# The last boot pass of V through the ordinary staging tiles, in the first one-layer steps, with a new instruction order

## The chip, the cores and the metric

One core of a Trainium2 chip runs the whole program. The metric is device time in microseconds (us), from one launch. The engines are PE (TensorE, matrix products), DVE (VectorE), ACT (ScalarE), POOL (GpSimd) and SP (SyncE, which here only issues transfers). DMA queues move data between HBM (device memory) and SBUF (on-chip memory); PE writes its results into eight PSUM banks.

## The reference

The input x has 2048 rows of 512 numbers. Two layers of attention with a recurrent memory (A) and a gated feed-forward (B) follow each other, both with the same weights:

```python
for s in range(n_seg):                       # 64 segments of 32 rows
    h = concat([mem, xs])                    # 8 memory rows and the segment's 32
    q, k, v = h @ Wq, h @ Wk, h @ Wv         # 32 heads of 128
    p = softmax(where(mask, q @ k.T * scale, -1e9))
    o = (p @ v) @ Wo
    mem = o[:8]                              # goes into the next segment
    outs.append(o[8:])
...
x = x + A(layernorm(x)); x = x + B(layernorm(x))   # B: (sigmoid(x Wg) * (x Wu)) Wd
x = x + A(layernorm(x)); x = x + B(layernorm(x))
```

## The kernel before

The memory rows make the 64 segments a chain. The kernel runs it in 70 steps: step t does segment t of layer 0 and, six steps later, segment t - 6 of layer 1, so that from step 6 to step 63 two layers share a step. Steps 0 to 5 have layer 0 alone and steps 64 to 69 layer 1 alone; these are the one-layer steps. A block is four segments; after each block of layer 0 its feed-forward (`ffn`) runs beside the steps, and its result feeds layer 1.

A step (`emit_step`) forms q and k for three heads at a time (L820), copies them out of PSUM, forms scores (L855), does the softmax in six groups of heads on DVE and ACT (L869 to L886: mask, maximum, subtraction, exponential, sum, reciprocal, product), transposes the probabilities (L898), multiplies with V (L925), and adds all heads through Wo in one bank (L943). The eight memory rows of the result go by a DVE copy (L961) into the tile hT of the next step, whose q and k wait for them. While there is no second layer, the first steps also form some columns of q and k for layer 1 in advance and save them through HBM (L849).

V does not depend on the memory for the rows of x, so it is formed in passes over 128 rows (`v_pass`, L609): eight pieces of 512 columns, each four 128x512 matmuls into one bank, a copy of the bank into a staging tile by ACT (L1176) or DVE (L1178), and writes of the staging tile to a scratch tensor `scr` in HBM (issued at L1172). A step reads its rows of V back into `vsb` (L789). What depends on the memory is formed in the step by strips (L734) and sent to `vsb` by L800. In an ordinary pass (`boot=False`) a piece goes to one of three tiles `vst` of 512 columns, and its writes are SP's. In a boot pass (`boot=True`) two pieces share a tile of 1024 columns from `bootp`, which borrows the nine ring tiles of the feed-forward weights (wd, wg, wu); its writes may go through SP or POOL, and the first loads of feed-forward weights wait for them (key "boot"). Seven boot passes of V, 56 pieces, run before and during step 0, for blocks 2, 14, 3, 4, 5, 7, 8, 10, 11 and 13 (`v_group`). The other blocks' rows of V come in beside the steps.

Boot also loads 16 MiB of weights (L496), whose transfers are issued by SP in one order with the rest of SP's work. SP and POOL have eight completion semaphores each: a transfer that takes one of them again waits for the one eight places earlier.

Nothing decides the order at run time. Every operation is recorded as a task with its dependencies; a packed table, `SEQUENCE`, gives the order of all tasks and, for tasks that may run on ACT or DVE (or SP or POOL), the engine. Then `replay` walks through this order with a table of costs, gives out tiles and banks, and sets the points of PE's work that the weight loads wait for; `warm` puts filler matmuls (L1162, on a tile of zeros) into PE where the plan leaves PE a gap over 250 ns near the start or in a stretch that is thinly filled with work.

Other lines of the profile: L569 transposes after a layer norm, L1013 the transpose ahead of a feed-forward, L1045 its gate and up products, L1068 its down product, L647 a half pass of V in boot.

Of the kernel before, what the change touches and what calls it, by code (L numbers as in the profile page):

```python
# [19 lines left out]
P = 128  # L20
MEM = 8
SEG = 32
L = MEM + SEG
# [3 lines left out]
NE = 14  # L27
# [26 lines left out]
;AzM!%Uu8nfB)KXVa0!tyA+v$awbu4`Kb`sD&qBM7uk$l2<aL9R`6B!jm=p6C^4)G&-1V@N>?u=U;*vtxzQ{<%y2d&u9DJ)U9CcRnC$6K!ij29MjC|~4KeQ93};?JQ7p@p1l)J*i!4g7+Bml0$ycMF-5YDdE_tMsZML)~cd?  # L54
}nJGL{`SyyT7;{fQ?*qBj!X1w_q9_L9p+-_rEfj(2^Qi4-0L<fxa6hdMklb>T@5A|k}ehjQ*{y5i=kgF8o(d{{O7GdF@Kj;J4s1vz-S*j?l1!WQ3b2G2#3Z{Rh*nyGO1@R-f_wKK51jA@8qwD~dF5X8VnzD0=Fe^+#pmy5m;
LUi$9=bhyZw14pl*t)pF}ga8SI9>}jO$Ym5Z_z(=ubg^h?&XJ1|QqZq_cZzLuzy#y;0H49pL`DshQU5fBlQ9Icc(z#Kb(Fa8W`fTYBvCvpLQ6*2e?+3ae9A(Nx;AUJ7YQxP8m$>Q-~uH~*4AYD><bXVJFPH4gH2_bXA!f424
@_r#~~-gm}MW;UejiWp{aJ)hi+l<6Ygrtd;7TKwO!xBySu(XZCrMjF7u`VA8t(jR!J{zR48z@Aiz$Lx>u=+Da|Nd@Jl@C!f9e6$s2{=Bom3p1|oAKY+p+<pV&Q?LU`v_4TZTh(Y*7k{uTw~)t889>{(ro!SoMr>PYU15#msZ
_}t+ek9rur<9#IIr?bpIJH!kkm1`@DI$;_#upVyKMH=^*}z36l&bjqmxJr<2*;@Y&`>sORISXA?*4Kh9}6>clU~Q*(Ztx-1Jo^LiJ>2)99=JGEZs{pR9wj?m6fv{5u6yJ=7B^Cg2-DU*XDS*q4ueJ*wl#L0OuF3gnn2@I2W|
I|9NbCrGR{Jip%xBqiFuV!Bf$3M6;LjF=W~UJH<g7`i1VZsE@R51DQH=IuLCb0}H4MUuI$tk4{EQMv@7i|pXc7{od_bJ!Z;@A?LZUj6-~nJg^Vw(q5xhy>fv4)%eRgl;}7W1feO6xvgFOVo@{Q<g$S!T41ZYWD8X{RWev3Zy
Ryh1AKtZJ}*M_d~*clQv!?_O(LhFXy4^Qy{g%b)re${{`K14VW+80jW^+%|bLlIPN{3#$&3*iV$hcYnMKO!1J+2V2B1-?Nwzxa@r+Mm#a>F?%b_X0C(3ljxJ!j7@`4ot+NL;c>g(MRO9?aJFC3a2Ho_!g$sV{WYL?Dkal!XV  # L60
@+^^eEU8<s#XnQjX*dw-{8J<gnvo|+_`w`?W7wu&vlEO%YqB(OaA}fFr87cMohwR1MpZ^*xOT0#NJhLsn&T>0d5v<eo!!}8XV9CdnF=U9mjeEnL!4(d7yZ_ybuRghPRU61x0_vQN?a;z1ZW7fSPMM?R0|&Xal0odTIy)MUXz
!bvxg-Ou0A5;&?tJxBc#?w=~3THxeKX1EHJ+?AzCG1r?&dIc$K9BsxIj9Zcc#LFncBB%GRpQ)KxBVCx|g-ENCrklW{MH*^IEXc_4`1V-jREC${Q3`gH*^=;P7?|&0H+hM>-HkZ{W%ztPn=z^-pEI7t?>6h+vGqOr6Rvuy4ft
40nPc@$uPvEosQ2Y|)nIKXK&rh{I&Uox}Xp@l}ND@z;eQp@H`^4M?0si?|>FM7a?7yYnOurV4#EoGevdai_XMK~SBs;eeQ5~(9z-V({bt18AG~n!isTDl8Msk-c0ADjgC0C3*@Lwuq0C>(sD}rOMj{g`;D(bSEs)wuVmckUp
47ma*F*bKwFl>YscB(?TVKo(g3kksEi%iB^E1;z@>i7Q%vz8u+FW?iy<}5d+I3sgF%xP^!tZnw|V-q;3=hAT82qj4r&re;vxN)T-GCRM$yI3WX!~7VHvgH!`8$?Y}G%kFMxT7_r*m89mwn(T&iKVdqcbmG|hgSzj_5|g{OJc
R(5d9!S3u|k+d&!DQb-K44Pe7Y`5o#evpE&KVqp*p4myYjmV`Gd3d{OPFkFJ*f=l;RVz1IB+&uXZK%RxX1!}UsW5X1gnspCdb`l4k*4T(kICd;vH3Zyr~Eq5|)@v=}{IAR{b+8@TVaS$JT+H&`VT<A*-9$4)n2zyJt+TqV^%
&r8W@^zu2WI>;NZiq15vYQx0;<C)fwd-H1a-`+j`h7}-l3x1|C9g`OGsFGRJN2yvDUU^Kx7u%@nR*J!6forss36zR+~{<;1WM(#<emy&6Jk$&m?iDL7Tt1<*)QN?B0mQ~3gQ+tNr{~(0b`g4<9N<DmOQEtE9G?A&A9q@Z3+`
#@HHeP5*_V#W%tQF#8^3A@APVUvQb0w=$uax&HuCqWt{+-5wWpr4@v{s-GYDc^^df-s41ZzUxpa{uQtm>FNGR!{g5n-VUB|x2@eZC>;+ubkKjE3D>|FuN;&;f@@Zs4MwdCIwVhk#=2eawi%w8jh$O(XZ{5TJk!25T4pgdm#m
zm54B6Y{`mGUuXP3*KW0w-P)f)#nXX@|I%cdQTW4tUYmtjn`()Uj3zf4HoC=Em|0y~KitYRDX24EI`drN7z>9+(;&Q^CzHl1#J=;DP{?QfsTEI+}7I3^z#zt>mq>j>+t_?66QS1nXMY@Ad_=HTt2jFm8~wA60Dvbny8*u3CN
8XmnU?X+LwX3ui2zXnF`bSu+yn5T>7>HT2<GC(Z5pXRTMs8w`PC)?$nA`3?3oz-KmdaQ(;env^f8ps5q7lkRR14}KCC_Mn2jAAn>TdiihS&6`L!3u_e6IYY62rL=CFm`8@T(gS^rBAYX<|x~<2RPtw`4{~KQOJ5GHc$W}Y`i
RRZg;<&k{>$m$cuPAft<?N+IN}Vahdk5Q+39I?~+x7E0~X0qV(0-T1l@{jg+^S@`^Bl%4!l}TCayYFH6GRY8?{1vu3oPUVbY74a2#l2r8Xg50WFBwe(4nGfp+799}_x-JxrZ5RMv<ciRxtB2;k6dDuo4>0zxTtyRY^+KE~<i  # L70
Y7eAJ3J{5XDKorFD&=Nbp{3pDcYUlE*1Go1~q@8ilQQ6I{-q!Z)KHnVYIV?3F9r!IdpY$NBlUNS}U5r8S3)IqMesa1o?qe)u&ujG6qY$<K|2mHo3)fU&RN&s5e_K7O{=_9z6UkN2K9ViA^krjvD$Irv;^oiMEUlbI-=G*Fp|
)3lv(5@bmv6cKn`3?%<$pV}@=g&$a@nlS=nHJZgg2)AlXrc*mV!#bQ(%j(}7p{wKV7Q7e*!pVj0WQ*OEEgKiaV8TV5+)?P7Y=y)P@lkOCdGucw4MhU|(y_Z~%W3TJGeTs#8Z&87JcrRX6(b>2pz0W>V|3}`d3{CRTSfQ;fNC
u%8OyxIJ89R~d<fCY3jx=~fe%avFoU-+!EP4A-)7Q7hl%Ak<D?&|yAD?78YFi=Ac$dc1K>5Mp(vOcS8u-P<_+}J^I3dWDopUxmaB~dOpw@l+>AUfT%Lm+Z4_XU@#p5|93`O^5+4{PHUPyDfasia4jqzozHQ6IHVAr|pHp1OV
mr!C?Dt8(P0bHn3oPsfsUZyANxTC-WGyIxKf}sEVJo{x*1A4O`O3Q<6YM9zEKRPeNZ^-nCG%z|oN;}h1PV2mVONn6Do_z+E90fa8`6s4t67mjA25kEvYYqo)6Jz|@kWdDOWHynvJraE`0gKYEnak+p#fPw;1qKRHk5Ou}(Sn
V78>^6>fFK2PqQ!(4_pN{&{C<s-n!<+1Vu#NOZf6z4wW3gqVMlBM`Vy>KnmLBZ_b4cYwMJj!P_p#FxX^SeZbO0|ac2YW)}8m*|N63&qv@DOra9i@?5l*njGHeZY9zmBwxku>Atv2FYO{ZHgDCof$X`@$subc&<5thxNrEePt
AudIJfh2W!CdP_KLPV5>~6>mN=!JEjZ_^?Y4!p<>BDvZL+O<jN@f00Mu1b^hSWR~6@mm4O7_>Gcc&a7X$#2Fw$)a)5L-Z314z8D+I0KfCFsQ+=2?YpWLhK#y{2Ia!JS+=Lm6mTw2xO;3FHvm5`34FeI-#B@A2z?wYX=ARxw_
tuU8@k{fr{Sv#bo>Ks?jgSsjAv`4DFOKn#VKjcu1tDl6w&PU|^<tJP?A&5l$ttcM6ID_N9j;;<WhQiw4_LXSBOeX11wz`70FI;cFy8~DROxYvx`b@MGwNs#1bU&pyd#a+<Xs3R#iO52d=-AB*d#Y^Aso1Jez3|PMaRj#COH;
j$tHfy;ya4~ZKc>T=`3oJwkZeD=T;z@<u{owk44ldXh%2iR6r&W231gX5+c0{M)49=*|_YDUr6-f~?YYbz0>pb}X5N5;XR0uSqAoxgU&`4^zJ}AFvfTW-Jl^DejXZ%iCCo_fxf4)pQY^8L6vDJ$x!?4Q;NqOKdbR}llga}&Q
@eZf>iaIQTN$S6A1e(DeM3KXW9R$jeJRw**TZS_+ZHJ0SCKRm;RU(r?51y~gO#_UJ=AvfX<CODs?AzSp#2@Jw8Weh;`Xw05k|8w%kWeWBkb(PDladC&@8Xi_At?H$TVx_1VDRzcNW#H3=pPLqZ{@V;3r6^idU9=U2QDycoCa
}X<;9E#ct(Zl!i5Ah`!104t8F2UlGY-aWLUe36yGaoQi9HIJIS~ZBtpEL_gL{cRne-!yMVsnL%kUF1tjZNAA(o!hj4mte1`ZPSs_ZWjP25@@Xc*@bg|<JslWe(&UFAz{yV(Lc&=-k{l0+Rw(aML&yWGi@U=v05n!X~4dEHN3  # L80
m95IPR`Aoo1;&d;XHy#!rlQZy}j#{(5htjIUq?0uP)lrfl7+`Xt4^f&W((|J(a!~11KdUbe3#G9ecttYzELIl@`Y_t-(t<57??;gSqPhA~-b$>FH;;&G8u6xHN+)OAn_aeS74l%s`TV1#otgP4`uCbaYkS*$wYD#-JIqA_P0
#1J5g+)l8UK7?&!3NizPK&S215c-|HTih11x?l3$m)#n7wLgw-7oQ#IyuKGzx8WyOf+DtpQ&s%y&PD(|r#(rw@s?44YCP$bJ0Po<HriBC3R~Qq|dRO-XA8y9ZQfC%)osl)<i&be@gKqatZK>(u4_|U@U<WWn#-tE*68Zi+<~
;sa1ky6+J{9Vj*YtYD3Tt)pzA^(E|HNwv6y2U8ZsLTHjF|=Zf#%6UkV<WLhOd;+Z1&F`_)t8ROVo_&EahI7xPY-GgQ(!n!|W=fn`Il6EGc?ngbb8FQ7?@xKhnyoC_e-?&*%>hY+>=|4yCasgBKR&8H+%LzD~kzqWwfXGsqD*
?1%6y!A8@Td&;#;U^SZ1^N`4T@)Z&3;oK(flk;5-c^%X^j!*~r4YY=jW5m#XE$QyDcWw*LEx%fv895eWw7Yg_JAe2rJhkz{ATZ&QGu`;*diH=ydnsA$BkIXPb^6p~(mz<j7rz9^k15#?N#N6qQKskAG85E>aB`r-2shNeRov
e=IMOZvfHg1t?EQ(of^BmUiwl<K!np`>y0se`d%^yn?f9+=kDcWb)XlTYcB~xTMlN@*-|wXZjJ%ki&MXd8-&bsOEoA5Mh=p+pjF^;rf~#WB@#nMKrVD!xV7&4&D1n8$nFJ&CGe;C$wyV=SHb)RQ7O_q|Q@xx{Ps>4B3)h|6Y
Z4*#cO$R)(t|Z|z<zv}FKZijIBcTHKjMi%CzRpCI;@mBit1}-SlP!sowvv`H!5$|qNK5RR*#~^EJtME+S!-vgll!5;7j9of>#1|$&IV(q0}(K0)sQ=4LW!&MFa&r0;Uxeu;;mC!|cEZnU*bjIQ&f{yTR-xadAP_4Ib+^s95P
558E(H5{&c2T7Vlh;oarLxWPacTwuKjuWPWSE}sFh(-J#V*T0QX`*Ar=g60>)+ZiXR>?W_ToSBx{&14#k;wm;Iu8@EosGYaBl$*NdM|rPTgeaoTEr?vIU*H`xIid@#h=%j@<6HkDB+Kn}-98p0+e?4=Z5CRdv6CB_XbTjB5U
i;}kKO-8kmg>@5<06G+sXnrIg9gV*mMFaZ5)2%F#q|fSNs8rv%-FcJ}LT<AyXtgYqV9~kUlxD{K_<Z5OVN0wLP?r0w+o4$Ze}~=Z9EMT7=yafzJusmAclbmz9TVpx~#`vb~@c{6GCIPz#{5y{+O6O50(IMNCIX+QI|IW_&SO
+te<Jgv>W3qhxtF<GhYBL?nVPgR|y>D>OZ})C3O_v;K<xYY~YB4pMPJ!saxrKUBmxQT)=o-U{cLdZO_U*uJPcA~$ypL_N#}E(GsT5!;fM;qOw=rP4MLGNYpawv#r=L}xfb_!<o(0__lO$V$<rWtLQKeML$J9(H0D5b@okfJm
LES-?xAA)ICmEgnLGL2Ul!9UZy@y*WXTv3Bp$1h-JP+cOEo>%Ghw39pQz(Hl|z@B6F`#Z&Q!Ff*#RIk|5#J~^mcX*5LeCV^p@j}JGOh3ppQeYTcZh##M1<W&f6*NS+K$<MymH5=zc|9)(`tWuiH>qc;C0s(g4ydoAm9ocdsu  # L90
;LR{N_AMqOq=@oM8DrR!sgqeF-~OAjvL4g!KI6e9EACK@~P*agJEaZcW~e4_g&w{EC031XLA70canUmHw@;xlOwboX6=wI@uapuHXE@9rZ}xZU#sn=%?P28Jd(X;oxMRenVnh^aq58De*FrUhT#$8Ze8~j$V%L+Y8SbR?c+7
Z#4_9Ze)n&=%)B9--_JpaimP1;FuCL1#!tCui?Y7;ocEmktl;)FYiKOz)R#;1RAHC;eR29gRrS-S{bIuNOxeoCn<BQ$tmbGFmKmANEb@O9=Ygqp+=ImkN?T;Oc?>fEm@LsGkuJy{3zYwQs@lnOTs1a^3FzYDfoz&Vs^Zmf{>
;>pp_mo7DJ5s4U~tlD`EC6<9m8$QSg?avq59L1S~Bv7w54MR3?$roWel+*c+#5N32_StS<|WhnK>XowbHXmAfQm*-XUY8hGQJRKFvg)Pw1HLCt!=mpp6zVv-tp(rEnQYbg_%zUX+@@{R(_gmDolu3KKHH3r`(T_z*{N8=VrA
#5^o2td_E)Gh&vJyBwFP5mG631|UN2le{`l6!>&1t~PiE{kEZ|Ho}f@y@W7{OPQC{dpR?sk8_c72tT>UnZ}dk8!xv5CyCidpIwTQ(R%s}R(&=#Hd*#(J60srdqHBaR<NGi;*r8tDhV28{~tCo!ZT`YTG_NJ)dhT)%$)^nvh<
# [266 lines left out]
class Kern:  # L361
# [312 lines left out]
    def v_group(self, blocks, psts, cuts):  # L674
# [5 lines left out]
        for b, cut in zip(blocks, cuts):  # L680
# [3 lines left out]
            for q, c0, r0, nr in cut:  # L684
                xi = (base + q) % 2
# [556 lines left out]
```

## Time and profile before

| | |
|---|---|
| median of 3 runs | 1766.37 us (1762.68 to 1766.64) |
| profiled execution, its own time | 1766.95 us |
| span in that profile | 1765.1 us |
| matmuls / weight loads recorded | 39831 / 40045 |
| granted TensorE clock, mean | 1.00 |
| bytes moved | 273.42 MB, mean 155 GB/s |

The page's first part gives each engine's busy time. A PE that is busy is not a PE at its peak: matmuls are pipelined, the ends are modelled, and fillers count as work. Rows of 512 columns have a mean of 379 ns each, but in a run of such matmuls one starts every 0.216 us; so a stretch's useful work is found from what runs of equal matmuls take, not from the mean of one. In the chain of waits each line gives the start in us, the duration in us and what the end of the program depended on at that time. A line such as "issue" means that the engine waited for nothing that the profile shows.

### The profile page before, as it was taken

What the parts mean: (1) busy time and instruction counts of PE and PEld (TensorE: products, weight loads), DVE (VectorE), ACT (ScalarE), POOL (GpSimd) and SP (SyncE); (2) the same over time, 40 slices, a digit from 0 to 9 for tenths busy, and PEclk for the clock granted to TensorE, in tenths of its full rate; (3) what the DMA queues carried; (4) which work ended last, traced back from release to release, by engine and by line L of the source; (5) the groups of instructions that cost most, each with busy time, mean ns of one, the idle gap of its engine ahead of it and who ended that gap; (6) DMA issues with size and microseconds to landing.
All of it is one profiled execution on the core that took longest, in us unless ns stands there. A gap on an engine that the chain in (4) does not pass through costs nothing.

```text
span 1765.1 us, 92070 instructions
## 1 busy us (share of the span) xinstructions
PE 1735.9 (98%) x39831; PEld 1505.6 (85%) x40045; DVE 1244.9 (71%) x4136; ACT 1103.3 (63%) x2906; POOL 573.8 (33%) x825
## 2 busy tenths in 40 slices
PE   9999999999999999999999999999999999999998
PEld 4588888889898888989898888988888898989887
DVE  5677677767677766776677778667766776677775
ACT  4576766566556656666666656656665666666564
POOL 4413032422333242323333242333324231333433
PEclk9999999999999999999999999999999999999999
DMA  9935364644555464545556464555456553554544
GB/s 310 313 81 140 103 173 134 180 137 132 161 150 164 134 175 143 152 123 158 170 141 175 125 181 112 156 160 160 141 144 178 147 155 111 162 160 140 171 127 118
DMA packets 135480, 273.42 MB, mean 155 GB/s; under 512 B 30730, under 2 KB 68498, under 8 KB 135074
## 3 DMA queue, kind: packets, MB, share of 16 engines
q0 software_dynamic: 56032, 181.39, 35.4%
q1 hardware_dynamic: 79042, 86.14, 17.0%
q8 instruction: 314, 5.14, 1.3%
q14 instruction: 92, 0.75, 0.1%
HBM read 221.78 MB, written 27.07 MB: 141 GB/s over the span
## 4 chain that ended last, share of the span: by engine, by line
PE 89%; DMA 4%; DVE 3%; SPq 2%; issue 1%; ACT 1%; DVEq 0%; POOL 0%; ACTq 0%
PE bank L820 31%; PE bank L943 17%; PE bank L1045 11%; PE bank L734 7%; PE bank L609 6%; PE bank L925 4%; PE bank L855 4%; PE bank L1068 4%; PE bank L898 2%; DMA wk_sb<-in_A_Wk_dram 1%; SPq L800 1%; DMA vsb<-sst 1%; PE bank L569 1%; SPq L496 1%; DVE st L869 1%
## 5 line engine op out<-in xcount | busy, mean ns | idle before, releaser
L820 PE MATMUL bank<-hT,wq_sb 128*128 128x80 bf16 (+3 forms) x8960 | 615.7, 198 | 3.0 <-issue 1.8
L820 PE MATMUL bank<-hT,wk_sb 128*128 128x80 bf16 (+3 forms) x8960 | 615.5, 198 | 2.5 <-issue 1.2
L1176 ACT CAST qku<-bank 128x480 bf16<-128x480 f32 (+3 forms) x770 | 383.8, 507 | 247.0 <-PE bank L820 218.5
L820 PEld LDWEIGHTS <-wq_sb 128*128 128x128 bf16 x8960 | 452.7, 99 | 32.3 <-issue 17.1
L820 PEld LDWEIGHTS <-wk_sb 128*128 128x128 bf16 x8960 | 447.0, 99 | 3.1 <-issue 1.8
L869 DVE TENSOR_TENSOR st<-bank,cst 40x240 f32<-40x240 f32 (+3 forms) x768 | 280.5, 368 | 129.1 <-PE bank L855 110.4
L943 PE MATMUL bank<-otsb,wo_sb 128*128 128x80 bf16 (+1 forms) x8960 | 362.8, 198 | 2.4 <-DMA wo_sb<-in_A_Wo_dram 1.3
L943 PEld LDWEIGHTS <-wo_sb 128*128 128x128 bf16 x8960 | 334.6, 99 | 11.1 <-DMA wo_sb<-in_A_Wo_dram 1.4
L1038 POOL DMA_DIRECT2D wu<-in_B_w_up_dram x217 | 164.6, 759 | 331.4 <-PE bank L1045 83.6
L1062 POOL DMA_DIRECT2D wd<-in_B_w_down_dram x217 | 154.2, 711 | 349.2 <-PE bank L855 102.6
L1176 ACT CAST otsb<-bank 128x480 bf16<-128x480 f32 (+3 forms) x420 | 201.1, 483 | 94.8 <-PE bank L925 62.8
L1037 POOL DMA_DIRECT2D wg<-in_B_w_gate_dram x217 | 164.3, 757 | 230.4 <-PE bank L1045 93.5
L879 ACT ACTIVATE st<-st 80x240 f32<-80x240 f32 (+3 forms) x420 | 159.1, 381 | 79.3 <-DVE st L876 76.8
L1045 PE MATMUL bank<-xnT,wg 128*128 128x128 bf16 (+2 forms) x1784 | 171.7, 218 | 1.0 <-issue 0.2
L1045 PE MATMUL bank<-xnT,wu 128*128 128x128 bf16 (+2 forms) x1784 | 171.2, 218 | 0.2 <-issue 0.2
L881 DVE TENSOR_REDUCE small<-st 80x6 f32<-80x240 f32 (+3 forms) x420 | 151.4, 362 | 23.8 <-ACT st L879 21.2
L855 PE MATMUL bank<-qku 128*128 128x80 bf16 (+1 forms) x2240 | 164.5, 197 | 1.1 <-ACT qku L1176 0.2
L876 DVE TENSOR_TENSOR st<-st,small 80x240 f32<-80x240 f32 (+3 forms) x420 | 154.7, 370 | 5.9
L886 DVE TENSOR_TENSOR pb<-st,small 80x240 bf16<-80x240 f32 (+3 forms) x420 | 153.7, 370 | 6.4
L874 DVE TENSOR_REDUCE small<-st 80x6 f32<-80x240 f32 (+3 forms) x420 | 152.1, 364 | 6.6
L925 PE MATMUL bank<-ptsb,vsb 104*128 104x80 bf16 x2048 | 140.6, 199 | 3.3 <-DMA vsb<-sst 0.9
L1051 DVE SCALAR_TENSOR_TENSOR hff<-th,bank 128x256 bf16<-128x256 f32 (+2 forms) x231 | 93.0, 403 | 62.8 <-ACT th L1049 62.3
(107 smaller groups left out, 2331.7 us busy)
## 6 DMA issues: line engine op xcount, KB each, us to landing
wg<-in_B_w_gate_dram POOLq DMA_DIRECT2D x220, 256.0 KB, 4.3
wu<-in_B_w_up_dram POOLq DMA_DIRECT2D x220, 256.0 KB, 4.2
wd<-in_B_w_down_dram POOLq DMA_DIRECT2D x220, 256.0 KB, 4.0
vsb<-scr SPq DMA_DIRECT2D x460, 48.0 KB
vsb<-sst SPq DMA_DIRECT2D x464, 32.0 KB
scr<-vst SPq DMA_DIRECT2D x112, 96.0 KB
wv_sb<-in_A_Wv_dram SPq DMA_DIRECT2D x8, 512.0 KB
wo_sb<-in_A_Wo_dram SPq DMA_DIRECT2D x10, 384.0 KB
```

Source lines behind the costliest of these rows:

```text
L820: nc.tensor.matmul(o_ap, lhsT=W[:, c, h * P:(h + 1) * P], rhs=mv(c), start=(c == 0), stop=(c == DC - 1))
L855: nc.tensor.matmul(s_all(SB)[:, w0 + i, :], lhsT=fview(qku[:, i, 0, 0:1], [(1, P)]), rhs=qku[:, i, 1, 0:ncol], start=True, stop=True)
L869: pl.add("DVE", dve_ns(n, True), lambda gsz=gsz, hs=hs, st=st, SB=SB, pj_=pj_, npj_=npj_, mk=mk, idx=idx: nc.vector.tensor_tensor(out=st[p ...
L876: pl.add("DVE", dve_ns(n), lambda gsz=gsz, hs=hs, st=st, mx=mx: nc.vector.tensor_tensor(out=st[pr, hs], in0=st[pr, hs], in1=mx[pr, hs].uns ...
L879: pl.add("ACT", act_ns(n), lambda hs=hs, st=st: nc.scalar.activation(out=st[pr, hs], in_=st[pr, hs], func=ACTF.Exp, scale=self.scale), r=s ...
L925: nc.tensor.matmul(fview(OB[:, o:o + 1], [(ncol, 2), (1, L)]), lhsT=self.vsb[halves[u // 8]][0:64 + L, j, (u % 8) * P:(u % 8 + 1) * P], rh ...
L943: nc.tensor.matmul(WB[:, c * ncol:(c + 1) * ncol], lhsT=self.wo[:, h, c * P:(c + 1) * P], rhs=otsb[:, hl, 0:ncol], start=(h == 0 and c == ...
L1037: pl.add("POOL", 760, lambda wg=wg, fs=fs: nc.gpsimd.dma_start(out=wg[:], in_=self.wgv[:, :, fs]), r=[("wo", self.H - 1)], w=[gk] + bt, la ...
L1038: pl.add("POOL", 760, lambda wu=wu, fs=fs: nc.gpsimd.dma_start(out=wu[:], in_=self.wuv[:, :, fs]), r=[("wo", self.H - 1)], w=[uk] + bt, la ...
L1045: nc.tensor.matmul(gu[:, 2 * i + k, 0:n], lhsT=W[:, c, i * P:(i + 1) * P], rhs=xnT[:, c, rw], start=(c == 0), stop=(c == DC - 1))
L1062: pl.add("POOL", 760, lambda wd=wd, ip=ip: nc.gpsimd.dma_start(out=wd[:], in_=self.wdv[:, 2 * ip:2 * ip + 2, :]), w=[dk] + (["boot"] if se ...
L1176: nc.scalar.copy(out=dst, in_=src)
```

## The change

The third pass of the last boot group (its rows come from blocks 11 and 13) becomes an ordinary pass: `v_group` takes a number `late`, and passes from that number on run with `boot=False`. Its eight pieces use `vst` tiles, SP alone issues their writes (sixteen of 512 columns in place of eight of 1024), and no feed-forward weight waits for them any more. `SEQUENCE` is replaced as a whole. In the new order the pass's eight pieces stand in steps 1, 2 and 3 (three, three and two), and the order of all other tasks, the choice between DVE and ACT and the places of the fillers differ throughout. The program has 41 filler matmuls where it had 71; PE's other 39974 matmuls are the same ones. 40 copies and scalings go from DVE to ACT.

```diff
 SEQUENCE = r"""
-;AzM!%Uu8nfB)KXVa0!t
...
 """
...
-    def v_group(self, blocks, psts, cuts):
+    def v_group(self, blocks, psts, cuts, late=9):
...
-                    self.v_pass(*args, True)
+                    self.v_pass(*args, q < late)
...
-        self.v_group([8, 10, 11, 13], {}, cuts)
+        self.v_group([8, 10, 11, 13], {}, cuts, 2)
```

## The prediction

> **What bounds the kernel now.** I read four views in this order: the page's totals and chain of waits, the busy time by stage, the chain in order of time, and the rows of the operations that the change moves.
>
> ```profile
> PE 1735.9 (98%) x39831; PEld 1505.6 (85%) x40045; DVE 1244.9 (71%) x4136; ACT 1103.3 (63%) x2906; POOL 573.8 (33%) x825
> ...
> PE 89%; DMA 4%; DVE 3%; SPq 2%; issue 1%; ACT 1%; DVEq 0%; POOL 0%; ACTq 0%
> ```
>
> PE sets the time, so this change can win only where PE does nothing useful. The stages, cut at the first q/k matmul of steps 1 to 4, at 240 and at 1640 us (columns: stretch, its length, busy us and count of PE, PEld, DVE, ACT, POOL, granted clock, DMA share, GB/s):
>
> ```profile
> 0.00:84.82 84.82, 79.22 (x836) 42.66 (x849) 51.56 (x145) 41.81 (x92) 37.13 (x85) 1.00 0.92 313
> 84.82:101.68 16.86, 16.60 (x495) 13.71 (x494) 13.16 (x51) 11.33 (x43) 3.04 (x6) 1.00 0.41 116
> 101.68:118.82 17.14, 16.25 (x497) 13.91 (x497) 12.12 (x47) 12.08 (x46) 2.94 (x4) 1.00 0.33 89
> 118.82:135.51 16.69, 15.92 (x492) 13.59 (x492) 11.40 (x43) 11.55 (x44) 1.42 (x2) 1.00 0.29 74
> 240.00:1640.00 1400.00, 1388.40 (x31614) 1233.64 (x31793) 996.78 (x3291) 887.24 (x2224) 460.57 (x636) 1.00 0.53 151
> ```
>
> The last row, 79% of the run, is 99% PE: nothing to win there. Boot and step 0 (first row) run with DMA at 0.92, and the chain there goes through weight loads:
>
> ```profile
> 32.00 12.33 DMA wk_sb<-in_A_Wk_dram
> ...
> 49.09 12.99 DMA wk_sb<-in_A_Wk_dram
> ...
> 73.69 9.88 DMA wo_sb<-in_A_Wo_dram
> ...
> 83.62 0.87 PE bank L943 x28
> 84.49 0.33 PE bank L1162 x2
> ```
>
> The end of step 0 is set by when the last part of Wo lands (83.6 us), not by PE. Steps 1 to 3 look 95% to 98% busy, but that includes fillers (L1162) and modelled ends. Their useful work, by paces in the chain (24 q/k matmuls in 0.61 us, 24 of Wo in 0.60, 32 strips in 1.84, three of L898 or L925 in 0.11), is 256 x 0.0254 + 128 x 0.025 + 1.84 + 32 x 0.025 + 32 x 0.037 = 13.5 us in a step of 16.9. In step 2 the hole is here:
>
> ```profile
> 107.84 0.40 DVE st L869
> ...
> 109.47 0.40 DVE pb L886
> ...
> 111.65 0.59 PE bank L1162 x2
> ```
>
> ```profile
> 107.80:111.70 3.90, 3.52 (x133) 3.42 (x129) 3.82 (x14) 2.99 (x11) 0.75 (x1) 1.00 0.35 76
> ```
>
> For 3.9 us the softmax of the single layer keeps DVE at 98%, and PE ends it on a filler.
>
> **The change, part by part.** In the program order a piece of V is four 128x512 matmuls (L609). Eight of them take 1.73 us in the chain, 0.216 each, so a piece is 0.865 us. Before, all 56 pieces of the seven boot passes stand ahead of step 1; after, 48 do, with three pieces in step 1, three in step 2 and two in step 3. So 8 x 0.865 = 6.9 us of PE moves.
>
> *Boot and step 0.* 6.9 us of PE and 1 MiB of writes to the V scratch leave. PE is not the limit there; the queue is. At the stage's 313 GB/s 1.05 MB is 3.35 us earlier for the last Wo load. Bounds: nothing, if that load is held by its place in SP's order (one late part ends the stage), and 6.9 if PE turns out to decide. I take 3.3, nearest to the DMA row. Fillers before step 1 grow from 26 to 32 matmuls (5.4 to 6.3 us); the transfers hide them, and if Wo came earlier still they would cost 0.9.
>
> *Steps 1 to 3.* They gain 6.9 us of V. Their 27 fillers (17 of 512 columns, 3 of 384, 4 of 256, 3 of 128, at 0.216 us per 512: 4.75 us) shrink to 2 (0.32). Net PE stream +2.5 us. Before, useful work and fillers were 3 x 13.5 + 4.75 = 45.3 of 50.7 us, so 5.4 us was plain waiting. If that stays, the steps lengthen by 2.5; if V falls exactly into it and 1.5 us is left, they shorten by 1.4. In the trace the fillers did not cover the holes (PE waits before some, 0.6 us the longest on DVE), so part is open: I take +0.4. Each piece also brings a copy and two writes:
>
> ```profile
> L1172 SPq DMA_DIRECT2D scr<-vst x224: 303/636/1552, 183.6 to 1512.1; - x112
> L1176 ACT CAST vst<-bank x82: 562/586/629, 183.7 to 1488.3; 128x512 bf16<-128x512 f32 x82
> L1178 DVE CAST vst<-bank x30: 673/682/693, 182.7 to 1495.0; 128x512 bf16<-128x512 f32 x30
> ```
>
> (count: shortest/median/longest ns, then first and last start.) In the new order ACT makes five of the eight copies, DVE three, all three around the start of step 3, while DVE would wait for that step's first scores; one stands ahead of the 0.2 us copy of memory into hT (L961) that starts step 3. DVE gets 3 x 0.682 = 2.05 us. Its idle time in step 3, 16.69 - 11.40 = 5.3 us, covers this; placed in the 98% stretch instead it would cost all 2.05. Nothing reads these V rows until the steps of blocks 11 and 13 (step 44 on), so no step waits for their arrival. The 16 writes are SP's alone, at 636 ns 10.2 us of its time, where eight larger ones went through SP or POOL. Behind them on SP stand the loads of V (L789, L800) and the q/k saves (L849); SP's slack in the steps covers them, and the price without it is the third rival. POOL issues seven fewer.
>
> *The new sequence elsewhere.* Fillers from step 4 to the last one-layer steps go from 7 to 4 (1.08 to 0.76 us), in the tail from 11 to 3 (1.84 to 0.49). Together 1.67 us leaves PE. If each hole remains, the gain is 0; if the surrounding waits shrink too, at most double, 3.3. I take 1.2. The DVE and ACT assignments shift too (40 instructions go from DVE to ACT); both have slack (71% and 63%) and I price this at nothing; without slack 40 copies at 0.1 us difference (0.682 - 0.586) would be 4 us on ACT or DVE, not on PE.
>
> *Instruction blocks.* PE stops inside runs of equal matmuls with no releaser:
>
> ```profile
> PE bank L820 <- issue: 3.0, 5, 1.0
> ...
> 1721.86 0.89 issue
> ```
>
> Counted in PE's instructions, the stops at 89.6, 160.1, 549.6, 1678, 1683, 1718, 1722, 1739 and 1744 us all fall at place 194 or 195 of a block of 256, and the queue of instructions moved 314 packets of 16 KB, one per 256. All but one lie in stages with few columns, where 128 matmuls pass in 3.2 us. After, the block holding the stop at 160 has 3.75 us of work (was 3.20), since other matmuls are mixed in; several in the tail still have 3.2 to 3.6. The waits view gives 4.5 us of issue time in all as the most to gain; new short blocks could cost as much as 2. I take 0.8 gained.
>
> The Trainium skill, Runtime: NRT & Kernel Launch, section Instruction fetch mechanics, says that the fetch runs ahead by itself and is hidden behind the sequencer's own pace. By that this term would be 0 and the sum 0.8 us later. The period of 256 and the 0.89 us row speak against it here.
>
> **The sum.** -3.3 + 0.4 - 1.2 - 0.8 = -4.9 us. The profiled execution took 1766.95 us (span 1765.1, 1.85 around it); less 4.9 is 1762.05. The median of the runs shown, 1766.37, is 0.6 below the profiled one, so 1761.4.
>
> **The rivals.**
> *The whole hole is used.* Boot is bounded by PE after all and gains the full 6.9 instead of 3.3, and the steps shorten by 1.4 instead of growing by 0.4: 5.4 better, 1756. For it: in boot DMA's share dips (SP waits on strips of step 0 ahead of the Wo loads), so a better order has something to win. Against it: a 0.92 share leaves 6.8 us of empty queue at most.
> *The cover moves with the work.* Wo keeps its landing time (0 instead of -3.3) and steps 1 to 3 pay all of +2.5 (2.1 more): 1761.4 + 5.4 = 1766.8, no change. For it: the DVE chain above waits for no PE work, so the steps need not shorten.
> *SP becomes the bound.* SP issues in order, and a write of a V piece waits for its copy; a load of the next step's V behind it comes late, and the P·V matmuls (L925) wait. Price: 16 x 0.636 = 10.2 us if every issue lands on the path; 1761.4 + 10.2 = 1771.6, slower than before by 5.2. It decides once more than 4.9 us of the 10.2 shows as waits of L925. For it: L925 already waits for loads of V (0.7 us in 84 to 240). Against it: DMA's share is only 0.29 to 0.41 in these steps.
> The Trainium skill, DMA: Bandwidth & Descriptors, section Rules for kernel authors, advises against this splitting: transfers under 64 KB are mostly overhead, and half the new ones are 32 KB. No row here times such a write to its landing; by the rule the third rival gains weight, and the 636 ns issue row, alike for 32 and 96 KB, is what its price rests on.
>
> **How the numbers follow.** Forecast 0.50, whole hole 0.19, cover moves 0.12, SP bound 0.19. Within about 0.3% (5.3 us, so 1761.1 to 1771.7) a measurement cannot tell a change. The forecast lies on the lower edge, so half of it is faster, half the same. Faster: 0.25 + 0.19 = 0.44; same: 0.25 + 0.12 = 0.37; slower: 0.19, as small new waits would carry the third rival past the edge. The forecast's own range is 1757 to 1766. The range, 1753 to 1772, takes in the rivals' values and 3 us below the best.
>
> **What would show it.** Right: the first q/k matmul of step 1 starts near 81.5 us (84.8 before), step 4's near 132.6 (135.5), with L609 matmuls where L1162 stood; the 240 to 1640 stretch is unchanged; fewer issue stops at period 256. Wrong: step 1 still starts at 84 us or later; L925 waits for vsb in steps 1 to 4; steps 1 to 3 together over 53 us; or the middle stage gains waits of its own, for which I allowed nothing.

## The result and the profile after

The changed kernel took 1758.3 us (median of 10 runs, 1754.2 to 1760.8), the kernel before 1766.5 us on the same chip (10 runs, 1761.5 to 1770.2): ratio 0.9958, 95% interval 0.9946 to 0.9970. By the ratio it is faster by 0.42%, 7.4 us; the medians are 8.2 us apart. The profiled execution took 1760.8 us (span 1759.0), 6.1 us less than that of before. Repeated on another chip, the ratio was 0.9973 (0.9964 to 0.9982), about 5 us: that is below.

PE's totals and the chain by engine, on the page of the changed kernel:

```profile
PE 1742.0 (99%) x40015; PEld 1503.4 (85%) x40015; DVE 1233.3 (70%) x4096; ACT 1113.6 (63%) x2946; POOL 570.8 (32%) x818
...
PE 94%; DMA 3%; SPq 1%; issue 1%; DVE 0%; ACT 0%; POOL 0%; DVEq 0%; POOLq 0%; ACTq 0%
```

DVE has gone from the chain (3% before), and PE stands for 94% of it (89%). That is not the change: second traces have 93% for PE and 1% for DVE in before, 90% and 3% in the changed kernel. The trace of before shown here and the second one of the changed kernel lack over 200 matmul records (of L609 and L1068), the other two none. The same stages as before, cut at the first q/k matmul of steps 1 to 4 and at 240 and 1640 us:

```profile
0.00:80.00 80.00, 74.76 (x823) 39.98 (x824) 46.10 (x137) 40.83 (x91) 31.67 (x73) 1.00 0.94 312
80.00:97.45 17.45, 17.24 (x495) 14.11 (x494) 11.94 (x45) 12.85 (x46) 4.39 (x8) 1.00 0.57 162
97.45:114.06 16.61, 16.60 (x497) 13.90 (x496) 13.21 (x48) 11.59 (x45) 2.09 (x3) 1.00 0.34 89
114.06:131.52 17.46, 16.65 (x493) 14.01 (x492) 14.20 (x49) 12.15 (x48) 2.77 (x4) 1.00 0.39 105
240.00:1640.00 1400.00, 1396.98 (x31791) 1233.06 (x31789) 987.72 (x3251) 892.98 (x2255) 460.86 (x635) 1.00 0.53 150
```

Boot and step 0 are 4.8 us shorter (80.0 for 84.8). Steps 1 to 3 take 51.5 us where they took 50.7, with 6.9 us more of V in them. (PE's 8.6 us more in the last row come with the missing records: this stretch has 31614 matmuls recorded before and 31791 after.) The chain in order of time (start, length, what):

```profile
35.46 13.68 DMA wq_sb<-in_A_Wq_dram
...
53.50 10.70 DMA wk_sb<-in_A_Wk_dram
...
78.25 1.42 PE bank L943 x56
79.66 0.23 PE bank L569 x4
80.00 2.51 PE bank L820 x96
```

The load of Wo that ended step 0 before (landing at 83.6 us, 9.88 us in the chain) is gone from it: the last 56 output matmuls (L943) run in one row, with no wait among them. Instead PE now waits for Wq and Wk earlier on, where it did not for Wq. From the waits of PE:

```profile
PE bank L820 <- issue: 4.0, 6, 1.6
PE bank L925 <- DMA vsb<-sst: 1.6, 3, 0.9
PE bank L820 <- DMA wq_sb<-in_A_Wq_dram: 1.5, 1, 1.5
PE bank L820 <- DMA wk_sb<-in_A_Wk_dram: 1.2, 1, 1.2
```

The hole of step 2 (3.9 us in which DVE was 98% busy and PE ended on a filler) is still a full stretch of DVE, but PE has V matmuls to do where the filler stood, one piece in this window and two right behind it:

```profile
103.50:107.50 4.00, 4.00 (x133) 3.52 (x131) 3.97 (x16) 3.75 (x16) 1.33 (x2) 1.00 0.35 65
```

```profile
106.42 0.87 PE bank L609 x4
...
107.88 0.86 PE bank L609 x4
...
109.12 0.86 PE bank L609 x4
```

Later the order cannot be read from one trace against one: by step 64 the lead has gone from 5.1 us at step 8 to 3.4, and the last matmul has 6.2. One part of this is a single stop of 1.6 us that ends at 440.1 us, which a second trace of this kernel, below, does not have.

### The profile page after: what moved, and what is told of

Its sections match the earlier page's. It is cut to its first block, busy times and chain, and to the rows that moved or that the text cites. A ratio compares the mean times of both kernels' runs of the same rounds, so it can differ in the third digit from the quotient of the medians.

```text
span 1759.0 us, 92161 instructions
## 1 busy us (share of the span) xinstructions
PE 1742.0 (99%) x40015; PEld 1503.4 (85%) x40015; DVE 1233.3 (70%) x4096; ACT 1113.6 (63%) x2946; POOL 570.8 (32%) x818
## 4 chain that ended last, share of the span: by engine, by line
PE 94%; DMA 3%; SPq 1%; issue 1%; DVE 0%; ACT 0%; POOL 0%; DVEq 0%; POOLq 0%; ACTq 0%
PE bank L820 33%; PE bank L943 17%; PE bank L1045 11%; PE bank L734 7%; PE bank L609 7%; PE bank L1068 6%; PE bank L855 4%; PE bank L925 4%; PE bank L898 2%; PE bank L569 1%; DMA wq_sb<-in_A_Wq_dram 1%; DMA vsb<-sst 1%; SPq L800 1%; DMA wk_sb<-in_A_Wk_dram 1%; PE bank L1013 0%
## 5 line engine op out<-in xcount | busy, mean ns | idle before, releaser
L1176 ACT CAST qku<-bank 128x480 bf16<-128x480 f32 (+4 forms) x770 | 383.5, 507 | 272.8 <-PE bank L820 244.5
L943 PE MATMUL bank<-otsb,wo_sb 128*128 128x80 bf16 (+1 forms) x8960 | 363.2, 198 | 0.6 <-issue 0.6
L943 PEld LDWEIGHTS <-wo_sb 128*128 128x128 bf16 x8960 | 335.1, 99 | 11.4 <-issue 1.3
L855 PE MATMUL bank<-qku 128*128 128x80 bf16 (+1 forms) x2240 | 160.7, 198 | 0.4 <-ACT qku L1176 0.4
L925 PE MATMUL bank<-ptsb,vsb 104*128 104x80 bf16 x2048 | 139.3, 199 | 2.2 <-DMA vsb<-sst 1.6
L855 PEld LDWEIGHTS <-qku 128*128 128x128 bf16 x2240 | 114.2, 99 | 30.1 <-ACT sst L1176 5.5
```

The lines of the kernel that those rows point to most:

```text
L855: nc.tensor.matmul(s_all(SB)[:, w0 + i, :], lhsT=fview(qku[:, i, 0, 0:1], [(1, P)]), rhs=qku[:, i, 1, 0:ncol], start=True, stop=True)
L925: nc.tensor.matmul(fview(OB[:, o:o + 1], [(ncol, 2), (1, L)]), lhsT=self.vsb[halves[u // 8]][0:64 + L, j, (u % 8) * P:(u % 8 + 1) * P], rh ...
L943: nc.tensor.matmul(WB[:, c * ncol:(c + 1) * ncol], lhsT=self.wo[:, h, c * P:(c + 1) * P], rhs=otsb[:, hl, 0:ncol], start=(h == 0 and c == ...
L1176: nc.scalar.copy(out=dst, in_=src)
```

## The experiments

Twelve kernels ran in three groups of four, each group on a chip of its own beside runs of before: medians of before 1760.8, 1759.0 and 1761.4 us, against 1766.5 on the chip of the result. So ratios are compared, not times. A new order of the same tasks needs a new sequence text, which can't be read; for these kernels the edit is given as what stands where in the order. "Old order" and "new order" are those of before and of the changed kernel.

The first table has the ratios to before on the same chip, with what that is in us.

| kernel | chip | ratio, 95% interval | us |
|---|---|---|---|
| before without later fillers | 2 | 1.0001, 0.9992 to 1.0009 | +0.2 |
| changed kernel without later fillers | 2 | 0.9984, 0.9975 to 0.9993 | -2.8 |
| old order, only the pass moved | 2 | 1.0028, 1.0017 to 1.0040 | +4.9 |
| before, pass in boot by the ordinary tiles, no later fillers | 2 | 1.0088, 1.0072 to 1.0104 | +15.5 |
| changed kernel again | 3 | 0.9973, 0.9964 to 0.9982 | -4.7 |
| new order to step 10, old from there | 3 | 0.9983, 0.9974 to 0.9992 | -3.0 |
| old order to step 12, new from there | 3 | 0.9990, 0.9982 to 0.9999 | -1.8 |
| pass moved, and three loads of Wo earlier | 3 | 1.0012, 1.0003 to 1.0021 | +2.1 |
| before, the pass with a quarter of its matmuls | 4 | 1.0008, 0.9999 to 1.0017 | +1.4 |
| before, the pass written twice | 4 | 1.0003, 0.9992 to 1.0013 | +0.5 |
| changed kernel, the pass with a quarter of its matmuls | 4 | 0.9975, 0.9965 to 0.9985 | -4.4 |

The second has the start of the first q/k matmul of steps 1, 4 and 8, read from the traces in us, one execution each.

| kernel | step 1 | step 4 | step 8 | steps 1 to 3 |
|---|---|---|---|---|
| before, first chip | 84.8 | 135.5 | 221.1 | 50.7 |
| before again, chip 4 | 83.0 | 134.8 | 221.0 | 51.8 |
| old order to step 12 | 82.6 | 133.2 | 218.4 | 50.6 |
| before without later fillers | 84.2 | 135.1 | 220.9 | 50.9 |
| changed kernel, first chip | 80.0 | 131.5 | 216.0 | 51.5 |
| changed kernel again | 82.1 | 132.8 | 216.4 | 50.7 |
| new order to step 10 | 81.9 | 132.5 | 215.9 | 50.6 |
| changed kernel without later fillers | 81.4 | 132.3 | 215.9 | 50.9 |
| changed kernel, quarter pass | 78.6 | 129.1 | 214.2 | 50.5 |
| before, quarter pass | 81.1 | 132.7 | 218.7 | 51.6 |
| only the pass moved | 84.9 | 140.3 | 228.3 | 55.4 |
| pass moved, three loads of Wo earlier | 81.6 | 136.4 | 221.0 | 54.8 |
| before, the pass written twice | 82.4 | 136.3 | 220.7 | 53.9 |
| before, pass in boot by the ordinary tiles | 99.2 | 153.2 | 238.2 | 54.0 |

One order's step 1 differs by 2 us and more between executions, so a difference of single traces of that size proves nothing alone. Four traces of the old order with the full pass in boot begin step 1 at 83.6 us on average, five with the new boot at 80.8: 2.9 us, of which the first pair, 4.8, showed a large case.

**Are the fillers on the path?** Both kernels were run with the warming matmuls of the cold start alone:

```diff
-                if cold or lo < 0.6 * self.SPAN:
+                if cold:
```

> The kernel before without its 58 warming matmuls that stand later than the cold start (71 become 13, 13.06 us of them become 2.80 us); what is computed stays the same. Theory 'waits': the fillers stand in waits whose ends something else sets, so the time stays 1766.5 us within 2 us, step 1 still begins near 84.5 us, step 4 near 135.2 us, and the 10.3 us come back as idle time of PE. Rival 'fillers are on the path': PE sets the end, the time falls by up to 10.3 us to about 1756 us, and step 1 begins about 2 us sooner. Rival 'clock': the granted clock falls under 1.00 in steps 0 to 3 and the time rises by 5 us or more.

> The changed kernel without its 28 warming matmuls that stand later than the cold start (41 become 13, 7.82 us become 2.80 us); PE then has the same matmuls as in the run of before without fillers. Theory 'waits': 1758.3 us within 2 us, and the distance between this kernel and before without fillers stays 6 to 8 us. Rival 'the gain is the 5.24 us of fillers that the new order has less': the two kernels without fillers come out within 2 us of each other, whatever their level.

Taking 10.3 us of fillers out of before left its time as it was (ratio 1.0001, within 1.6 us either way): they stand in waits that something else ends, and step 4 began at 135.1 us as ever. Granted clocks stayed at 1.00 in steps 1 to 3 without them. In the changed kernel nothing was gained either. Its distance to before without fillers, 0.17% or 3 us, is under the 6 to 8 that I wrote down from the first chip; with half-widths of 0.09% for each ratio the distance is 3.0 us give or take 2.2, so the two do not come out alike, though the rival's 2 us is not shut out by this pair alone. That the 5.2 us of fewer fillers are not the gain follows from the first run: before paid nothing for its own.

**The move alone.** The last pass through the ordinary tiles, its pieces, copies and writes in steps 1 to 3 about where the new order has them; all else in the old order. Seven of the eight pieces stand in steps 1 to 3; one is left in boot, and its writes, too, come after step 1 has begun (86 us).

> The order of before for everything but the last boot pass: its eight pieces, copies and 16 writes stand in steps 1 to 3 where the changed kernel has them, through the ordinary staging tiles; nothing else is re-ordered (81 warming matmuls, 15.3 us, against 71). Theory 'the move is the gain': step 1 begins near 79.7 us as in the changed kernel (before 84.5), steps 1 to 3 then take 50.7 to 52.5 us, and the end comes out 3 to 5 us under before, 1761.5 to 1763.5 us; the rest of the changed kernel's gain (about 3 us) is the re-annealed order after step 4. Rival 'the move is given back': without a re-annealed order the pieces push the work of steps 1 to 3 aside, step 4 begins at 135 us or later, and the time is 1766 us or more. Rival 'all of it is the move': 1758 us.

The rival came: slower by 0.28%, and step 1 begins at 84.9 us although 6.0 us of PE work had left boot and the pass is written after it. SP's transfers of this kernel, around the end of boot (start, length, what):

```profile
62.45 3.87 SPq L800 DMA_DIRECT2D vsb<-sst  x4
66.36 9.53 SPq L496 DMA_DIRECT2D wo_sb<-in_A_Wo_dram  x10
```

The last ten loads of Wo stand on SP behind four copies into vsb (L800), and the first of these waits, by the chain, for a DVE copy (kx, L1178) that follows the q/k matmuls of step 0. SP of before has the same order there:

```profile
63.08 2.70 SPq L800 DMA_DIRECT2D vsb<-sst  x4
65.83 10.40 SPq L496 DMA_DIRECT2D wo_sb<-in_A_Wo_dram  x10
```

By stretches, for the kernel with the move alone (columns as above, the last two DMA share and GB/s):

```profile
64.00:68.00 4.00, 4.00 (x25) 1.91 (x24) 3.24 (x13) 1.76 (x5) 0.00 (x0) 1.00 0.58 147
...
80.00:84.00 4.00, 1.42 (x43) 1.32 (x44) 0.00 (x0) 0.40 (x2) 0.92 (x2) 0.87 0.92 337
```

While SP waits, the queue runs at 147 GB/s; then all ten loads come at once, and PE, with nothing else left, is busy 1.4 of the last 4 us, until the chain's load of Wo (9.72 us long) lands at 83.3. The same hole is in before again:

```profile
64.00:68.00 4.00, 3.93 (x34) 1.93 (x30) 2.99 (x10) 2.43 (x10) 0.00 (x0) 1.00 0.50 146
```

Taking work out of boot made the wait longer, not the boot shorter: PE waits 3.4 us for Wo at the end of boot, for 1.3 us in the first trace of before. In steps 1 to 3 the pieces were simply added: 55.4 us for 50.7 (the granted clock of step 1 is 0.96, a small part of it). By the matmuls in program order, PE's work there is 49.7 us (45.0 before), so 5.7 us is waiting, as much as before; only 1.35 us of fillers gave way.

**The order of SP.** The same kernel, three of the ten loads earlier on SP:

```diff
-vsb<-scr, vsb<-scr, scr write, vsb<-sst x4, wo x10
+wo x3, vsb<-scr, vsb<-scr, scr write, vsb<-sst x4, wo x7
```

> The order of before with only the last boot pass moved (the kernel that came out at 1766.4 us with step 1 at 84.7 us), and three of the ten late loads of Wo taken on SP's queue ahead of the copies that wait for the first q/k results. Theory 'Wo's loads hold the boot': the move took the PE work and the writes out of boot, but the last load of Wo was issued when SP came past those waits, at 66 to 76 us, and landed at 83.3 us; with 1.2 MB of it ahead of the waits the last lands 2 to 3.5 us sooner, step 1 begins at 81 to 82.5 us, and the end comes out 2 to 3.5 us under the kernel with the move alone. Rival 'bytes': the queue is full anyway, the last load lands at 83 us as before, and step 1 stays at 84 to 85 us.

SP's transfers and two stretches of this kernel:

```profile
58.65 4.07 SPq L496 DMA_DIRECT2D wo_sb<-in_A_Wo_dram  x3
64.62 4.29 SPq L800 DMA_DIRECT2D vsb<-sst  x4
69.66 3.58 SPq L496 DMA_DIRECT2D wo_sb<-in_A_Wo_dram  x7
```

```profile
64.00:68.00 4.00, 3.70 (x34) 1.93 (x31) 2.98 (x9) 2.43 (x9) 0.00 (x0) 1.00 1.07 393
...
80.00:84.00 4.00, 4.00 (x151) 3.75 (x148) 1.00 (x3) 1.94 (x6) 2.23 (x5) 1.00 0.99 328
```

The hole is filled (393 GB/s for 147), PE is busy to the end of boot, step 1 begins at 81.6 us, and the ratio falls by 0.0016, 2.8 us, as the theory said. The two kernels ran on two chips, each beside before, so the 2.8 us are uncertain by 2.6: the direction is shown, the size hardly. Steps 1 to 3 still take 54.8 us, so this kernel stays slower than before. The new order does the same more thoroughly, with five loads of Wo from 57.4 us and six from 65.7:

```profile
57.42 7.69 SPq L496 DMA_DIRECT2D wo_sb<-in_A_Wo_dram  x5
65.16 0.52 SPq L800 DMA_DIRECT2D vsb<-sst  x1
65.72 5.24 SPq L496 DMA_DIRECT2D wo_sb<-in_A_Wo_dram  x6
```

**What a byte and a matmul cost in boot.** Before once more for a trace on the same chip, before with a quarter of the last pass's matmuls, and before with the pass's eight writes issued twice, the second time to a spare region:

```diff
-                for c in range(DC):
...
+                for c in range(1 if pieces[-1][2] == 13 else DC):
...
```

```diff
+                if pieces[-1][2] == 13:
+                    d2 = self.spare[b * BLK * XS:(b + 1) * BLK * XS, ps]
...
                     {"SP": nc.sync, "POOL": nc.gpsimd}[tk.on].dma_start(out=got[1], in_=got[2])
+                    if got[0] is not None and not isinstance(got[0], str):
+                        {"SP": nc.sync, "POOL": nc.gpsimd}[tk.on].dma_start(out=got[0], in_=got[2])
```

> Before itself once more, for a second trace of it on the chip of the next three kernels. On the second and third chips before has run at 1760.8 and 1759.0 us, and a kernel with its order up to step 12 began step 1 at 82.4 us where the first trace of before has 84.5 us. If that spread is the chip's or the execution's, step 1 begins between 82 and 84.5 us here and the stops at the period of 256 PE instructions, some 6.2 us in all in the first trace, come to another sum (the changed kernel's came to 6.3 us on one chip and 2.7 us on another). If both are the kernel's own, step 1 begins at 84.5 us again and the stops at 89.6, 160.1, 1722.5 and 1744.5 us come back with the same lengths.

> Before with the last boot pass cut to one of its four matmuls for each piece, still in boot (of that pass's values only the first quarter of the sum over D is computed; copies and writes stay): 24 matmuls of 216 ns, 5.2 us of PE work less before step 1. Theory 'the loads of Wo end boot': PE waits for the last load of Wo instead, step 1 begins 0 to 1.5 us sooner and the end comes 0 to 1.5 us sooner. Rival 'PE ends boot': step 1 begins and the kernel ends about 5 us sooner.

> Before with each of the eight writes of the last boot pass issued twice on its queue, the second time to a scratch region that nobody reads: 1.05 MB and eight issues more in boot. Theory 'bytes' (the prediction's term, 1.05 MB at 313 GB/s): step 1 begins and the kernel ends about 3.3 us later. Rival 'the queue has holes that Wo's late issue leaves': step 1 begins 0 to 1.5 us later.

Neither costs what its size says. 5.2 us of PE work less gave 1.0008 (at best 0.2 us faster). Step 1 of this one trace begins 1.9 us before that of before again, but nothing of that is left in the medians. PE then waited for Wo, which ends step 0 in the chain of the quarter pass:

```profile
70.72 9.15 DMA wo_sb<-in_A_Wo_dram
79.92 0.95 PE bank L943 x28
```

In before again the chain goes through 56 matmuls of L943 in one row at 81.34 us, without a wait for Wo: there PE ended step 0. Of the four traces of this boot with the full pass, PE waited for Wo at its end in two, for 1.3 and 0.4 us. So PE's work and Wo's landing ended boot within 2 us of each other, and taking one away leaves the other.

The second writes gave 1.0003, at most 2.3 us, where 1.05 MB at 313 GB/s would be 3.3. But this run puts only half of them into boot: they are issued from 71.9 to 89.1 us, four of the eight after step 1 has begun (82.4). The pass's own writes stand no better. By their places in the order of SP and POOL, which the two kernels share, they start, in the first trace of before, at 72.3, 77.5, 77.6, 81.6, 83.2, 84.6, 84.7 and 85.8 us, while Wo's ten loads are issued from 65.8 to 76.2 and the last lands at 83.6. So one write of the eight, 0.13 MB, goes out ahead of the last load of Wo, and four more start before it lands. The 1.05 MB that the move was to take from in front of that load never stood there as a whole.

The later second writes fall into step 1, which takes 20.0 us in this trace, for 17.9 in before again. Its chain has a stop of PE that nothing releases, and from 94 to 98 us the granted clock is 0.59:

```profile
91.03 2.42 issue
```

Steps 4 to 7 are 1.9 us shorter in this trace than in before again, so nothing of it is left by step 8 (220.7 us for 221.0). Whether the writes lengthened the stop, one trace does not show.

**The pieces in steps 1 to 3.** The changed kernel with the same cut of the pass.

> The changed kernel with the moved pass cut to one of its four matmuls for each piece, in steps 1 to 3 (of that pass's values only the first quarter of the sum over D is computed; copies and writes stay): 5.2 us of PE work less in these steps. Theory 'the pieces stand in waits' (the prediction's +0.4 us for steps 1 to 3): steps 1 to 3 take 0 to 1.5 us less than the 50.7 us they took in the changed kernel on the last chip, and the end comes 0 to 1.5 us sooner than the changed kernel's 0.9973 of before. Rival 'PE sets steps 1 to 3': they take 45.5 us and the ratio falls to 0.994.

Steps 1 to 3 took 50.5 us with 5.2 us less of PE work, where they took 50.6 to 51.5 with all of it, and the ratio is 0.9975 (0.9973 with all of it, on chip 3): the pieces stand in waits. In the new order PE's work in these steps is 47.4 us. It replaced 4.4 us of fillers and some 2 us of waiting.

**Head and tail of the order.** The changed kernel itself; its order up to step 10 with the old one behind; the old order up to step 12, with the pass in boot and the old staging, and the new order behind.

> The changed kernel itself once more, beside the other runs of this chip: on this chip before has run at 1760.8 us and before without fillers at 1761.0 us. If the fillers cost nothing here too, the changed kernel comes out where it did without fillers, 1757.9 us within 1.5 us (ratio 0.9984), and its step 1 begins 3 to 5 us sooner than that of before. If its gain on the first chip was its fillers or a thing of that chip alone, the ratio is 1.000 or, as there, 0.9958 (1753.4 us).

> The order of the changed kernel up to the first matmul of step 10, and the order of before from there on. Theory: the gain is the head's (boot and steps 1 to 9), so step 8 begins about 215.5 us (before 220.8) and the end stays 4 to 5 us under before. Rival: the tail's order gives half of it; then step 8 begins as early, but only 1 to 3 us are left at the end.

> The order of before up to the first matmul of step 12, the last boot pass in boot as before, and the order of the changed kernel from there on. Theory: the tail's order alone changes nothing that can be told, within 1.5 us of before, step 8 at 220.8 us. Rival: the new tail gains 2 to 3 us by itself (1758 us where before has 1760.8), from step 64 on.

-3.0 and -1.8 us add up to the -4.7 of the whole. Neither interval reaches 1, though the second nearly does, and the expectation that all of it would be the head's was too simple. By these medians some 60% is, but each part is uncertain by about 1.5 us. Within the head, the means of the second table (quarter passes left out) put the new order 2.4 us ahead at step 4 and 4.3 at step 8. So steps 4 to 7 may matter as much as boot: 83.4 to 84.5 us in the new order, 85.2 to 86.2 in the old. The other traces blur this: the changed kernel with the quarter pass took 85.1 us there, and the old order took 84.4 and 84.6 in the kernels with the pass written twice and with three loads earlier. Waits that are seen there in the old order are a stop of PE without a releaser near 160 us and, in the trace with the quarter pass that lacks this stop, waits of L925 for vsb (1.9 us); the new order has no stop over 0.5 us in that stretch. That these make the difference is not shown.

The changed kernel again came out lower (0.9973) than without fillers on another chip (0.9984); the intervals overlap, so this shows no use of the fillers.

**The staging alone.** Before with the pass left in boot, but through the three ordinary tiles and 16 writes on SP, without later fillers.

> Before with the last boot pass left in boot, but through the three ordinary staging tiles with 16 writes of 512 columns on SP in place of 8 of 1024 columns on SP and POOL; no warming matmuls later than the cold start, so it stands against before without these fillers. Theory: staging alone brings nothing, since the 1.05 MB still cross in boot: step 1 begins at 84.5 us or up to 5 us later, and the time lies 0 to 6 us over the run of before without fillers. Rival 'staging is what frees the boot': step 1 begins 2 us or more sooner than in before without fillers.

Slower by 0.88%, 15.3 us over before without later fillers by the two ratios (16.9 by the medians), over two and a half times the upper end of what I expected. The waits of 60 to 100 us in this kernel:

```profile
ACT vst L1176 <- DMA scr<-vst: 10.5, 1, 10.5
PE bank L609 <- ACT vst L1176: 9.8, 1, 9.8
```

A copy waits 10.5 us for a tile, since that tile's last write stands on SP behind the loads of Wo, and PE, whose order has the next piece there, waits 9.8 us for the copy. The last load of Wo stands behind twelve of these writes in turn and is issued at 94.7 us. Step 1 begins at 99.2 us, 15.1 later than without; steps 1 to 3 take 54.0 us for 50.9, at a granted clock of 0.82 in the first two. In this order three tiles with writes on SP did not serve a pass in boot, where nine with a second queue did. So here the ordinary tiles go with the pieces leaving boot.

## Why the prediction came out as it did

The sum was -4.9 us and 1761.4 us; measured were -8.2 on the first chip, -4.7 on another. The time is in the range, and the direction is that of the larger part of the chances. But its steps were right in size more than in reason, and that the sum came so near is in part luck: two of its terms were not found, and gains that it did not have stand in their place.

*Boot and step 0, -3.3 by bytes.* Size right: 2.9 us over these nine traces, 4.8 in the first pair (step 1 at 80.0, 81.5 forecast). The step that failed is "PE is not the limit there; the queue is", with the bytes at 313 GB/s as price. Seven of the pass's eight writes go out behind the last load of Wo in before, and three only after it has landed, so their bytes were not what it waited for; and without them and 6.0 us of PE work step 1 came no earlier. The lower bound I wrote, "nothing, if that load is held by its place in SP's order", was the mechanism, and moving loads of Wo ahead of SP's waits brought 2.8 us, give or take 2.6. The reannealed sequence did that; the diff of the code does not show it, the order of SP's instructions did.

*Steps 1 to 3, +0.4.* Right within the spread of the traces: 50.6 to 51.5 us in the new order, 50.6 to 51.8 in the old. The quarter pass shows that the pieces are hidden. But they are hidden by the order, not by the place: with the old order around them seven of the pieces cost 3 to 5 us.

*Other fillers, -1.2.* Wrong: fillers cost nothing (10.3 us of them, ratio 1.0001). The bound of 0 was the answer.

*Instruction blocks, -0.8.* Mis-sized, and not a fixed number. PE's stops at place 194 or 195 of 256 sum to 3.6 us in the first trace of before and 4.9 in that of after, to 4.8 and 1.6 in the second traces. The section on the hardware says why this can't be priced from one trace.

*Tail and middle.* I allowed nothing but fillers and blocks for them. The new order from step 12 on gives 0.10%, 1.8 us (0.2 to 3.2 by its interval), for which the sum had no term.

*The rivals.* "The whole hole is used" (1756) came near on time and was wrong on PE: PE did not end boot alone. What was written for it, that SP waits on step 0 ahead of the Wo loads, was the right place to look. "The cover moves with the work" is what the move alone did, in boot and in steps 1 to 3 both; the new order avoids it. "SP becomes the bound" did not come for the 16 writes: in steps 1 to 3 L925 waits 0.2 us in all for vsb. Its price was also too high: the 636 ns are the middle of two kinds of write, and in the trace of before the 112 of 96 KB take 0.35 us and the 112 of 32 KB 0.69 us to issue, so not alike; sixteen sum to 8.3 us. SP was a bound already, in boot, through the order of its queue.

What stays open: whether the loads of Wo moved ahead in before, with the pass left in boot, would gain by themselves, and whether an order annealed again without the move would gain as much. Neither was run. No kernel here beat the changed one.

## What to carry to other kernels

Where two chains end a stage within a few us of each other, price neither from its own length: taking PE work away gave nothing here, and taking away both PE work and writes gave nothing either. Before a queue's bytes are put in the sum, see which of them are issued ahead of the transfer that matters. Look, too, for stretches in which it is half empty, and for the waiting instruction that its next large loads stand behind; three loads moved past such a wait filled such a stretch here and gained 2.8 us, give or take 2.6. And a change that moves work into holes holds only with the order that leaves the holes there, so moving it and ordering it again are to be judged together.

## What the runs showed of the hardware

*The stops of PE differ between executions of the same order.* They come at the same instructions, not with the same length. The rows that follow such a stop near 160 us, from the timeline of PE (in brackets the idle time before), in before, before again, and the old order to step 12:

```profile
160.39 0.25 PE L820 MATMUL bank<-hT,wq_sb 128*128 128x54 bf16 x3 [0.98 <-issue]
```

```profile
155.75 0.20 PE L820 MATMUL bank<-hT,wk_sb 128*128 128x54 bf16 x1 [0.79 <-issue]
160.30 0.25 PE L820 MATMUL bank<-hT,wq_sb 128*128 128x54 bf16 x3 [1.17 <-issue]
```

```profile
157.88 0.25 PE L820 MATMUL bank<-hT,wq_sb 128*128 128x54 bf16 x3 [1.09 <-issue]
```

The stop of about 1.1 us is there each time, at the same matmul; the one of 0.79 us a block earlier is in one trace alone. With 48 PE instructions fewer ahead of it (the quarter pass) the block ends elsewhere in the work, and no stop of 0.23 us or more is left near it. Counted by PE's idle time, the stops of 0.23 us and more at places 194 and 195 of 256 that nothing releases sum to 3.6, 4.8 and 1.7 us in these three traces, and to 4.9 and 1.6 us in two of the changed kernel. (The sums of 6.2, 6.3 and 2.7 in the expectation above come from another count.) Single traces of one order thus differ by 3.3 us in this alone; the medians of before on the four chips spread over 7.5. The Trainium skill, Runtime: NRT & Kernel Launch, section Instruction fetch mechanics, has blocks of 256 instructions, as here, and calls the crossing mostly hidden; here one crossing took up to 1.2 us in these rows and 2.4 in the kernel with the pass written twice, and a run has up to 4.9 us of them.

*A short wait can halve PE's clock, or not.* In the new order PE waits for Wk near 64 us. Afterwards, in the changed kernel on the first chip and then on the third (four matmuls to a row):

```profile
64.24 0.27 PE L820 MATMUL bank<-hT,wk_sb 128*128 128x54 bf16 x4 [1.25 <-DMA wk_sb<-in_A_Wk_dram]
64.35 0.26 PE L820 MATMUL bank<-hT,wq_sb 128*128 128x54 bf16 x4
64.45 0.26 PE L820 MATMUL bank<-hT,wk_sb 128*128 128x54 bf16 x4
```

```profile
64.91 0.28 PE L820 MATMUL bank<-hT,wk_sb 128*128 128x54 bf16 x4 [1.66 <-DMA wk_sb<-in_A_Wk_dram]
65.03 0.33 PE L820 MATMUL bank<-hT,wq_sb 128*128 128x54 bf16 x4
65.17 0.36 PE L820 MATMUL bank<-hT,wk_sb 128*128 128x54 bf16 x4
65.35 0.36 PE L820 MATMUL bank<-hT,wq_sb 128*128 128x54 bf16 x4
```

Rows start 0.10 us apart in the one and 0.18 in the other, until 68.5 us; the granted clock from 64 to 68 us is 1.00 and 0.63. About 20 rows at 0.08 us more are 1.6 us, which is most of the 2.1 us between the two starts of step 1. Three of five traces of this boot show it (0.63, 0.69, 0.65), two do not, one of them after the least busy stretch of all (PE busy 1.80 of the 4 us from 60 to 64). Step 1 begins at 81.4 to 82.1 us in the three and at 78.6 and 80.0 in the two.

The clock records of the traces say what decided. Within each of the seven traces in which the clock changes on the way, these changes lie on a grid of 3.413 us. I cut all fourteen traces by this grid, up to the last 20 us, and summed the columns of the matmuls that begin in each interval (some 8100 would fill one, at 0.216 us for 512). The 16 intervals with 3072 columns or fewer are each followed by one at half clock; none of the 7115 with 3152 or more is. The interval that holds the wait for Wk has 1564, 1890 and 2430 columns in the three traces, and 3694 and 3618 in the two. So it is the work done in a fixed interval that counted here, not the length of a wait.

The Trainium skill, TensorE: Matmul & The Clock Gate, section Part 1: The HAM clock gate, has the clock decided in windows of about 3.4 us that run on by themselves, and the half clock come after an idle one. The windows agree with the grid. That the window must be idle does not: at 2430 columns PE had done almost a third of what fills it.
